# Moving the fifth shifted reading of a bit-trick exp from VectorE to GpSimd, timed beside VectorE's PSUM reads

## The chip, the cores and the metric

The kernel runs on one core of a Trainium2 chip. The metric is the device time of one execution in microseconds (us), lower is better. TensorE is called PE, VectorE DVE, ScalarE ACT and GpSimd POOL in the profile lines.

## The reference

A transformer block with adaptive layer norm: 2048 tokens, width 512, 32 heads of width 16, then a GELU layer of width 1376.

```python
x = A_x                                                  # [1, 2048, 512] bf16
mod = silu(c) @ w_mod                                    # six vectors of 512
h = layernorm(x) * (1 + ca) + sa
q, k, v = split_heads(h @ wqkv, 32)                      # heads of width 16
p = softmax(q @ k.T / 4)                                 # 32 heads, 2048 x 2048 each
x = x + ga * (merge(p @ v) @ wo)
h = layernorm(x) * (1 + cb) + sb
x = x + gb * (gelu(h @ w1 + b1) @ w2 + b2)
```

What matters is the softmax: 32 x 2048 x 2048, or 134 million exponentials, against matmuls of a narrow head width.

## The kernel before

The work is cut into 32 runs. In each, 16 key tiles of 128 keys meet 4 heads x 512 queries. PE computes scores into PSUM in two halves of 128x1024; then each key tile takes one of two ways.

- On ScalarE ("A" tiles): two exps of 128x1024, and then one group of PE products with V.
- On VectorE ("D" tiles): one addition that turns the score into the bits of a bf16 power of two, stored as a 16-bit integer. That is a coarse exp. To smooth it, the integers are also read with four different offsets added ("shifted readings", `sh`, 128x2048), and PE multiplies each of the five readings with its own scaled copy of V. A D tile therefore costs five groups of PE products instead of one.

```python
NPH = 5                                          # readings of a D tile
PH_SH = [round(128 * j / NPH) for j in range(NPH)]       # 0, 26, 51, 77, 102
DKS = (2, 6, 10, 14)                             # key tiles of a run that may go to VectorE
...
def exp_a(qk, r, kt, half):                      # ScalarE
    def go(o):
        n_a[1] += 1
        nc.scalar.activation(out=o.tile, in_=qk.tile, func=ACT.Exp, scale=ESC)
    e = op("ACT", go, 0.92, (qk,), lat=AL, prio=1.0, acq=r_pt, rel=(qk,))
    ...
def exp_d(qk, r, kt, half):                      # VectorE
    first = o_ph[0]
    def go(o):
        n_d[1] += 1
        dst = first.tile[:, half * 2 * QB:(half + 1) * 2 * QB]
        nc.vector.tensor_scalar(out=dst, in0=qk.tile, scalar1=PH_B, scalar2=0.0,
                                op0=ALU.add, op1=ALU.max)         # PSUM -> int16
    e = op("DVE", go, 1.14, (qk, before), lat=DL, prio=0.5, rel=(qk,))
    ...
    pv_op(r, kt, 0, (e,), parts(first), (first,))
    for j in range(1, NPH):
        sh = op("DVE", lambda o, j=j: nc.vector.tensor_scalar(
            out=o.tile, in0=first.tile, scalar1=PH_SH[j], scalar2=None, op0=ALU.add),
            0.6, (e,), lat=DL, prio=2.0, acq=r_sh, rel=(first,))
        pv_op(r, kt, j, (sh,), parts(sh), (sh,))
```

The program contains its own planner. Every operation is given an assumed duration (0.92, 1.14 and 0.6 us above). The planner lists the operations in the order in which they could start by these durations, and emits a fixed instruction order for every engine. Each engine works through its own order and waits at semaphores. So a wrong duration cannot give a wrong result, but it can give an order that does not fit the chip.

Other work sits in the same orders. GpSimd normalises each finished run (`OT`, 128x512), computes the reciprocal standard deviations of the layer norms (`rs`), and scales V for the D tiles (`VX`). VectorE evicts PSUM; PE does the projections and the feed-forward layer. Score buffers `st` are three, exp outputs `pt` nine, D tiles `ph` three, shifted readings `sh` four.

The softmax here doesn't subtract the row's maximum and nothing guards it: scores larger than these inputs give would overflow.

Of the kernel before, what the change touches and what calls it, by code (L numbers as in the profile page):

```python
# [11 lines left out]
ALU = mybir.AluOpType  # L12
ENG = mybir.EngineType
# [58 lines left out]
class Op:  # L72
    count = 0

    def __init__(self, eng, fn, us, deps=(), lat=0.14, prio=5.0, mode=None, kind="", acq=None,
                 rel=(), gate=None):
        self.eng, self.fn, self.us, self.lat, self.prio = eng, fn, us, lat, prio
        self.mode, self.kind, self.acq, self.rel, self.gate = mode, kind, acq, rel, gate
        self.end = None
        self.ready = 0.0  # L80
        self.tile = None
        self.slot = None
        self.kb, self.due, self.extra = 0, 1e9, False
        self.uses = 0
        self.waiters = []
        self.todo = 0
        self.seq = Op.count
        Op.count += 1
        for d in deps:
            if d is None:  # L90
                continue
            if d.end is None:
                d.waiters.append(self)
                self.todo += 1
            else:
                self.ready = max(self.ready, d.end)
        for owner in rel:
            owner.uses += 1


class Plan:
    SLACK = {"PE": 0.10, "DVE": 0.05, "ACT": 0.15, "POOL": 0.05, "SP": 0.05}

    def __init__(self, dyn, later):
        self.later, self.fill_at, self.cool, self.heat, self.until = later, 0.0, 0.0, None, 1e9
        self.free = {e: 0.0 for e in self.SLACK}
        self.lists = {e: [] for e in self.SLACK}
        self.mode, self.tiles, self.now = None, {}, 0.0
        self.bus = 0.0
        self.dyn, self.done, self.fill = dyn, deque(), FILL  # L110

# [13 lines left out]
    def start(self, op):  # L125
        s = max(op.ready, self.pe_start(op) if op.eng == "PE" else self.free[op.eng])
        if op.acq is not None:
            s = max(s, min(op.acq.free))
        if op.eng == "PE" and self.later(op):
            s = max(s, self.fill_at)  # L130
        return s

# [12 lines left out]
    def ahead(self, can):  # L145
# [6 lines left out]
        for s, o in can:  # L152
            end = s + o.us + (0.107 if o.mode[0] != "qk" else 0.0)
            if o.kind == "qkA" or end <= limit:
                keep.append((s, o))
        return keep

    def commit(self, s, o):
# [25 lines left out]
        else:  # L184
            self.free[o.eng] = s + o.us
        o.end = s + o.us + o.lat
        if o.kb:
# [34 lines left out]
def kernel(  # L222
# [29 lines left out]
    ESC = math.log(2.0) / 128.0  # L252
    DKS = (2, 6, 10, 14)
    NPT = 9
    FEW = 2
    MM = 512 / 2400.0
    FIRST_D, D_TIME = 1, 6.0

# [69 lines left out]
    def op(eng, *a, **k):  # L328
        o = Op(eng, *a, **k)
        if eng == "PE":  # L330
            o.due = due_now[0]
            due_now[0] += due_now[1]
        return plan.add(o)
# [179 lines left out]
    def layer_norm(src, deps, mod, mod_dep, hold_z, alloc_h, engines, ps_res, kind, prio,  # L513
# [4 lines left out]
              for t in range(nt)]  # L518
# [3 lines left out]
        za = [op("DVE", lambda o, t=t: apply(ln, z, t, src(t)), 0.33, (z, rs[t // 2]), prio=prio,  # L522
                 rel=(ln,)) for t in range(nt)]
        h = op("POOL", None, 0.0, (rs[0],), lat=0.0, prio=0.0, acq=alloc_h)
# [70 lines left out]
    def make_v(b, cc, kind, acq, eng):  # L595
# [16 lines left out]
        for t in DKS:  # L612
            if t // TPB == b:
# [4 lines left out]
                def scale(o, t=t, vf=vf):  # L618
                    for ph in range(1, NPH):
# [3 lines left out]
                            scalar2=0.0, op0=ALU.mult, op1=ALU.add)  # L623
                got.append(op("POOL", scale, 5 * 0.3, (vf, o_v0[b]), prio=1.0, rel=(vf,)))
        o_v[(cc, b)] = got
# [51 lines left out]
    def qk_op(which):  # L677
# [27 lines left out]
        if which == "D" and half == 0:  # L705
            o_ph[0] = op("POOL", None, 0.0, (), lat=0.0, prio=0.0, acq=r_ph)
        o = op("PE", go, MM, ([o_ph[0]] if which == "D" else []) + [evs[par or 0]] + [o_k[(cc, kb)]], lat=PEL, mode=("qk", half),
               kind="qk" + which, acq=r_st, rel=(qm,),
               gate=(lambda: n_a[0] - n_a[1] < 2) if which == "A" else
               (lambda: n_d[0] - n_d[1] < 2))  # L710
        (exp_a if which == "A" else exp_d)(o, r, kt, half)

    live = {"A": 0, "D": 0}

    def exp_a(qk, r, kt, half):
# [5 lines left out]
        if half == 1:  # L721
            lo = o_e.pop((r, kt, 0))
            o_e.pop((r, kt, 1))
            pv_op(r, kt, 0, (lo, e), lambda: [lo.tile, e.tile], (lo, e))

    def exp_d(qk, r, kt, half):
# [9 lines left out]
        if not half:  # L736
            o_e[(r, kt, 0)] = e
            return

        def parts(o):  # L740
            return lambda: [o.tile[:, h * 2 * QB:(h + 1) * 2 * QB].bitcast(BF16) for h in range(2)]
        pv_op(r, kt, 0, (e,), parts(first), (first,))
        for j in range(1, NPH):
            sh = op("DVE", lambda o, j=j: nc.vector.tensor_scalar(
                out=o.tile, in0=first.tile, scalar1=PH_SH[j], scalar2=None, op0=ALU.add),
                0.6, (e,), lat=DL, prio=2.0, acq=r_sh, rel=(first,))
            pv_op(r, kt, j, (sh,), parts(sh), (sh,))

    def pv_op(r, kt, ph, deps, srcs, owners):
# [43 lines left out]
        o.last_left = lambda: left[r]  # L793
        plan.add(o)

# [5 lines left out]
    def normalise(r):  # L801
# [20 lines left out]
        def d5(o):  # L822
# [5 lines left out]
            out=o.tile, in0=OD.tile, in1=o5.tile, op=ALU.mult), 1.3, (o5,), prio=0.5, acq=r_OT,  # L828
            rel=(OD, o5))

# [83 lines left out]
    def block_tail(b, nt=TPB):  # L914
# [8 lines left out]
        for t in range(nt):  # L923
# [9 lines left out]
                out=x2.tile[:, t, :], in0=y.tile, in1=xr.tile[:, t, :], op=ALU.add), 0.33,  # L933
                (m, xr), prio=1.5, rel=(y,)))
        h, hd, za, trs = layer_norm(lambda t: x2.tile[:, t, :], res_done, modB, o_late["mB"],
# [17 lines left out]
        for t in range(nt):  # L953
            first = None
            for lo, hi in ((0, 4), (4, 8), (8, NF)):
# [11 lines left out]
                out=o.tile, in0=y.tile, in1=x2.tile[:, t, :], op=ALU.add), 0.33,  # L967
                (m, o_late["gb"]), prio=1.5, acq=r_o, rel=(y, x2))
            dma(lambda o, t=t, a=a: nc.sync.dma_start(
# [219 lines left out]
```

## Time and profile before

| | before |
|---|---|
| time, median of 2 runs | 835.43 us (835.25 to 835.62) |
| exps on ScalarE | 778 of 128x1024 |
| PSUM reads for D tiles on VectorE | 246 of 128x1024 (123 tiles) |
| shifted readings on VectorE | 492 of 128x2048 |
| GpSimd busy | 12% |

The page of the profile for the kernel before. Its first part gives busy us, the share of the span and the number of instructions of each engine. The second cuts the span into 40 slices, each digit the busy tenths of one slice; PEclk is the granted PE clock in tenths of full speed. The fourth follows the chain of work that ended last.

```profile
PE 765.7 (91%) x8349; PEld 289.5 (35%) x8430; DVE 770.5 (92%) x1118; ACT 767.8 (92%) x816; POOL 98.4 (12%) x207
...
ACT  3799999898999999999999999999999999998942
POOL 4530221200002100000001100000001000010010
PEclk9999999998999999999999999999999999999999
...
DVE 32%; PE 30%; ACT 29%; issue 7%; DMA 1%; POOL 0%; SPq 0%; POOLq 0%; DVEq 0%; ACTq 0%
```

Busy time by window, kernel before (columns: window, its length, then busy us and number of instructions of PE, PE's weight loads, DVE, ACT and POOL; granted clock, DMA share, GB/s).

```profile
0.00:60.00 60.00, 50.91 (x428) 24.03 (x434) 37.75 (x90) 39.19 (x47) 25.02 (x126) 1.00 0.34 106
60.00:800.00 740.00, 685.67 (x7733) 251.08 (x7810) 714.97 (x995) 715.77 (x753) 71.82 (x78) 0.99 0.09 25
800.00:838.00 38.00, 29.11 (x198) 14.38 (x193) 17.75 (x34) 12.84 (x19) 1.59 (x4) 0.99 0.04 15
```

Three engines are nearly full for 740 us: ACT 96.7%, DVE 96.6%, PE 92.7%. The chain that ended last is split almost evenly among them. GpSimd has hundreds of free microseconds. The change wants these.

Instructions in order of time, kernel before, from 594 us on (columns: start us, duration us, engine, line, operation, output<-inputs, shapes, count, and in brackets the idle time before it and what ended it).

```profile
594.17 0.69 DVE L744 TENSOR_SCALAR sh_9491<-ph_9287 128x2048 int16<-128x2048 int16 x1
...
594.69 1.30 POOL L827 TENSOR_TENSOR OT_9532<-OD_9313,RB_9454 128x512 bf16<-128x512 f32 x1 [21.65 <-DMA RB_9454<-rn]
...
594.77 1.77 DVE L744 TENSOR_SCALAR sh_9502<-ph_9287 128x2048 int16<-128x2048 int16 x1
```

A shift usually takes 0.69 us. The one that begins 0.08 us after a GpSimd normalisation takes 1.77 us: it waits about until GpSimd has ended (594.69 + 1.30 = 595.99) and then needs its own time (it ends at 594.77 + 1.77 = 596.54). All 14 shifts over 0.9 us in this trace overlap or touch such a normalisation. The Trainium skill, "SBUF — State Buffer", section "SBUF: two separate sides", gives the reason: VectorE in a two-port mode and GpSimd share one pair of SBUF ports, and one excludes the other. VectorE's reads of PSUM show no such delay (246 reads, longest 1.23 us).

### The profile page before, as it was taken

How to read it: one execution, taken by the hardware profiler on the slowest of the kernel's cores; microseconds unless marked ns; L12 is line 12 of the kernel's file. 1: busy time of each engine (PE TensorE's matmuls, PEld its weight loads, DVE VectorE, ACT ScalarE, POOL GpSimd, SP SyncE). 2: the span in 40 equal slices, each digit the busy share in tenths (PEclk: the TensorE clock that was granted, in tenths of full speed). 3: DMA queues.
4: the chain of work that ended last, by engine and by line, in shares of the span. 5: the costliest groups of instructions: out<-in, count | busy, mean ns of one | idle time of the engine just before them, and what ended most of it. 6: DMA issues, size and time to landing. Idle time of an engine off the chain costs nothing.

```text
span 837.9 us, 20068 instructions
## 1 busy us (share of the span) xinstructions
PE 765.7 (91%) x8349; PEld 289.5 (35%) x8430; DVE 770.5 (92%) x1118; ACT 767.8 (92%) x816; POOL 98.4 (12%) x207
## 2 busy tenths in 40 slices
PE   8889999999999998998999898999999999999987
PEld 3433333332233332323233332223244444344443
DVE  7849999898999999988999999999999999999982
ACT  3799999898999999999999999999999999998942
POOL 4530221200002100000001100000001000010010
PEclk9999999998999999999999999999999999999999
DMA  6304101001100000000100000000100001000100
GB/s 201 101 1 112 27 16 41 5 23 54 41 15 14 16 15 14 16 20 21 40 16 14 16 14 16 8 28 20 40 15 16 10 12 37 16 28 22 42 7 26
DMA packets 31621, 25.07 MB, mean 30 GB/s; under 512 B 13773, under 2 KB 26926, under 8 KB 31530
## 3 DMA queue, kind: packets, MB, share of 16 engines
q1 hardware_dynamic: 31002, 23.78, 10.2%
q8 instruction: 66, 1.08, 0.5%
q14 instruction: 25, 0.20, 0.1%
q10 hardware_dynamic: 528, 0.00, 0.0%
HBM read 21.16 MB, written 2.61 MB: 28 GB/s over the span
## 4 chain that ended last, share of the span: by engine, by line
DVE 32%; PE 30%; ACT 29%; issue 7%; DMA 1%; POOL 0%; SPq 0%; POOLq 0%; DVEq 0%; ACTq 0%
PE od_13287 L775 1%; DMA blk_178<-in_w_mod_dram 1%; DVE ln_s L485 1%; PE od_11221 L775 1%; PE od_7486 L775 1%; PE od_12207 L775 1%; ACT g_10994 L949 1%; ACT g_7641 L949 1%; ACT g_4693 L949 1%; PE od_5604 L775 1%; PE od_2171 L775 1%; PE od_8961 L775 0%; PE od_10719 L775 0%; PE od_3379 L775 0%; ACT L718 0%
## 5 line engine op out<-in xcount | busy, mean ns | idle before, releaser
L775 PEld LDWEIGHTS <-VEB_92 128*32 128x32 bf16 x640 | 16.5, 96 | 15.8 <-issue 12.7
L775 PEld LDWEIGHTS <-VEB_91 128*32 128x32 bf16 x640 | 16.3, 96 | 16.1 <-issue 12.5
L775 PEld LDWEIGHTS <-VEB_89 128*32 128x32 bf16 x640 | 16.2, 97 | 15.9 <-issue 11.4
L775 PEld LDWEIGHTS <-VEB_90 128*32 128x32 bf16 x640 | 16.4, 96 | 14.4 <-issue 10.5
L942 PEld LDWEIGHTS <-W_83 128*128 128x128 bf16 x176 | 14.1, 97 | 20.3 <-issue 11.5
L700 PEld LDWEIGHTS <-kT_0_121 32*128 32x128 bf16 x128 | 8.0, 91 | 20.6 <-issue 20.1
L700 PEld LDWEIGHTS <-kT_0_109 32*128 32x128 bf16 x128 | 7.0, 91 | 20.0 <-issue 17.8
L700 PEld LDWEIGHTS <-kT_1_122 32*128 32x128 bf16 x128 | 7.0, 91 | 19.2 <-issue 18.7
L700 PEld LDWEIGHTS <-kT_0_113 32*128 32x128 bf16 x128 | 6.6, 91 | 19.1 <-issue 18.7
L700 PEld LDWEIGHTS <-kT_0_117 32*128 32x128 bf16 x128 | 7.0, 91 | 17.8 <-issue 17.2
L700 PEld LDWEIGHTS <-kT_1_114 32*128 32x128 bf16 x128 | 6.3, 91 | 19.7 <-issue 19.1
L700 PEld LDWEIGHTS <-kT_2_111 32*128 32x128 bf16 x128 | 6.8, 91 | 18.3 <-issue 16.5
L700 PEld LDWEIGHTS <-kT_2_123 32*128 32x128 bf16 x128 | 7.1, 91 | 17.2 <-issue 16.8
L700 PEld LDWEIGHTS <-kT_2_119 32*128 32x128 bf16 x128 | 6.9, 91 | 17.6 <-issue 17.3
L700 PEld LDWEIGHTS <-kT_2_115 32*128 32x128 bf16 x128 | 7.0, 91 | 17.2 <-issue 16.3
L700 PEld LDWEIGHTS <-kT_1_110 32*128 32x128 bf16 x128 | 6.8, 91 | 17.8 <-issue 15.4
L700 PEld LDWEIGHTS <-kT_3_120 32*128 32x128 bf16 x128 | 6.6, 91 | 17.7 <-issue 17.1
L700 PEld LDWEIGHTS <-kT_1_118 32*128 32x128 bf16 x128 | 6.3, 91 | 18.6 <-issue 18.2
L700 PEld LDWEIGHTS <-kT_3_124 32*128 32x128 bf16 x128 | 7.3, 91 | 14.8 <-issue 14.3
L700 PEld LDWEIGHTS <-kT_3_112 32*128 32x128 bf16 x128 | 7.0, 91 | 15.7 <-issue 14.3
L700 PEld LDWEIGHTS <-kT_3_116 32*128 32x128 bf16 x128 | 6.4, 91 | 15.1 <-issue 14.3
L501 ACT ACTIVATE blk_292<-st_327,modA 128x512 bf16<-128x512 bf16 x2 | 1.4, 774 | 9.1 <-PE st_327 L533 9.1
(4858 smaller groups left out, 3145.6 us busy)
## 6 DMA issues: line engine op xcount, KB each, us to landing
W_83<-in_B_w_dram SPq DMA_DIRECT2D x1, 1376.0 KB
g_1005<-in_w_mod_dram SPq DMA_DIRECT2D x2, 512.0 KB
xb_127<-in_A_x_dram SPq DMA_DIRECT2D x4, 128.0 KB
blk_174<-in_w_mod_dram SPq DMA_DIRECT2D x1, 512.0 KB
blk_178<-in_w_mod_dram SPq DMA_DIRECT2D x1, 512.0 KB
w_201<-in_A_wqkv_dram SPq DMA_DIRECT2D x1, 512.0 KB
w_205<-in_A_wqkv_dram SPq DMA_DIRECT2D x1, 512.0 KB
xb_210<-in_A_x_dram SPq DMA_DIRECT2D x1, 512.0 KB
```

The lines of the kernel that those rows point to most:

```text
L485: nc.vector.bn_stats(out=st6, in_=src)
L501: nc.scalar.activation(out=dst, in_=src, func=ACT.Identity, bias=mod[:, j:j + 1], scale=mod[:, NC + j:NC + j + 1])
L700: nc.tensor.matmul(out=o.tile[:, g * QB:(g + 1) * QB], lhsT=kT[cc][kb][rows, ko * P:(ko + 1) * P], rhs=qm.tile[rows, par, :] if hb is None ...
L775: nc.tensor.matmul(out=o_od[r].tile[32 * i:32 * i + 32, n * HB:n * HB + w], lhsT=v_tile(kt, ph)[:, c0:c0 + 32], rhs=got[i // 2][:, at:at + ...
L942: nc.tensor.matmul(out=o.tile[:, 0:N], lhsT=W1[:, j, f * P:(f + 1) * P], rhs=h.tile[:, j, 0:N], start=(j == 0), stop=(j == NC - 1))
L949: ge = op("ACT", lambda o: nc.scalar.activation(out=g.tile[:, :, 0:N], in_=g.tile[:, :, 0:N], func=ACT.Gelu_apprx_tanh), 0.1 + 1.2 * nt + ...
```

## The change

The intent: take the fifth reading of each D tile (0.60 us of VectorE) to GpSimd, in two halves of 128x1024. Begin each half only beside a VectorE read of PSUM, which does not need the shared ports and lasts 1.2 us. The plan counts on 1.05 us for a half. With the VectorE time won, up to five instead of four key tiles of a run may go to VectorE, so that ScalarE has fewer exps.

```diff
-    DKS = (2, 6, 10, 14)
+    DKS = (2, 5, 8, 11, 14)
-    FIRST_D, D_TIME = 1, 6.0
+    FIRST_D, D_TIME = 1, 8.0
+    POOL_US, POOL_MIN = 1.05, 0.95
...
+    def piece(first, last, n, e):
+        cols = slice(n * 2 * QB, (n + 1) * 2 * QB)
+        return op("POOL", lambda o: after_dve(nc.gpsimd.tensor_scalar(
+            out=last[0].tile[:, cols], in0=first.tile[:, cols], scalar1=PH_SH[-1], scalar2=None,
+            op0=ALU.add)), POOL_US, (e, last[0]), lat=0.2, prio=1.0, kind="beside", port=True,
+            rel=(first,), gate=lambda: plan.beside(POOL_MIN) or no_more_d())
...
-        for j in range(1, NPH):
+        for j in range(1, NPH - 1):
             sh = op("DVE", ...)
+        two = [piece(first, last, 1, e)]
+        pv_op(r, kt, NPH - 1, [last[1], two[0]], parts(last[0]), (last[0],))
...
+    def after_dve(pool):      # the half waits for the VectorE instruction before the PSUM read
+        own = [i for i in islice(reversed(nc.cur_bb.bb.instructions), 400) if i.engine == ENG.DVE]
+        if len(own) > 1:
+            tc.add_manual_dep(pool.ins, own[1].name, ..., reason="beside")
...
-               gate=(lambda: n_a[0] - n_a[1] < 2) if which == "A" else
+               gate=a_may if which == "A" else
+    def a_may():              # no second score ahead for ScalarE while VectorE waits for one
+        back = n_a[0] - n_a[1]
+        if back >= 1 and live["D"] and n_d[0] == n_d[1]:
+            return sum(f < plan.now for f in r_st.free) > 1
+        return back < 2
```

More of the change, by code (lines that the diff above doesn't have):

```diff
@@ L1 @@
 from collections import deque
+from itertools import islice
 from contextlib import ExitStack
@@ L75, in __init__ @@
     def __init__(self, eng, fn, us, deps=(), lat=0.14, prio=5.0, mode=None, kind="", acq=None,
-                 rel=(), gate=None):
+                 rel=(), gate=None, port=False):
         self.eng, self.fn, self.us, self.lat, self.prio = eng, fn, us, lat, prio
+        self.port = port
         self.mode, self.kind, self.acq, self.rel, self.gate = mode, kind, acq, rel, gate
@@ L109, in __init__ @@
         self.bus = 0.0
+        self.port = {"DVE": 0.0, "POOL": 0.0}
+        self.dve = (0.0, 0.0, True)
         self.dyn, self.done, self.fill = dyn, deque(), FILL
@@ L130, in start @@
             s = max(s, self.fill_at)
+        if op.port and op.us > 0:
+            s = max(s, self.port["POOL" if op.eng == "DVE" else "DVE"])
+        if op.kind == "beside":
+            s = max(s, self.dve[0])
         return s
@@ L156, in ahead, with beside @@
         return keep
+    def beside(self, us):
+        at, end, port = self.dve
+        t = max(at, self.now, self.free["POOL"])
+        if t >= end:
+            nxt = self.pick("DVE")
+            return nxt is None or nxt[0] - t >= us
+        return not port and end - t >= us
     def commit(self, s, o):
@@ L185, in commit @@
             self.free[o.eng] = s + o.us
+            if o.port:
+                self.port[o.eng] = s + o.us
+            if o.eng == "DVE":
+                self.dve = (s, s + o.us, o.port)
         o.end = s + o.us + o.lat
@@ L522, in layer_norm @@
         za = [op("DVE", lambda o, t=t: apply(ln, z, t, src(t)), 0.33, (z, rs[t // 2]), prio=prio,
-                 rel=(ln,)) for t in range(nt)]
+                 rel=(ln,), port=True) for t in range(nt)]
         h = op("POOL", None, 0.0, (rs[0],), lat=0.0, prio=0.0, acq=alloc_h)
@@ L623, in scale @@
                             scalar2=0.0, op0=ALU.mult, op1=ALU.add)
-                got.append(op("POOL", scale, 5 * 0.3, (vf, o_v0[b]), prio=1.0, rel=(vf,)))
+                got.append(op("POOL", scale, 5 * 0.3, (vf, o_v0[b]), prio=1.0, rel=(vf,), port=True))
         o_v[(cc, b)] = got
@@ L724, in exp_a @@
             pv_op(r, kt, 0, (lo, e), lambda: [lo.tile, e.tile], (lo, e))
+    d_last = [None]
+    def piece(first, last, n, e):
[4 more added lines that the diff above has]
+            rel=(first,), gate=lambda: plan.beside(POOL_MIN) or no_more_d())
     def exp_d(qk, r, kt, half):
@@ L737, in exp_d @@
             o_e[(r, kt, 0)] = e
+            to = op("POOL", None, 0.0, (e,), lat=0.0, prio=0.0, acq=r_sh)
+            d_last[:] = [[to, None]]
+            d_last[0][1] = piece(first, d_last[0], 0, e)
             return
@@ L742, in exp_d, with no_more_d @@
         pv_op(r, kt, 0, (e,), parts(first), (first,))
-        for j in range(1, NPH):
+        for j in range(1, NPH - 1):
             sh = op("DVE", lambda o, j=j: nc.vector.tensor_scalar(
                 out=o.tile, in0=first.tile, scalar1=PH_SH[j], scalar2=None, op0=ALU.add),
-                0.6, (e,), lat=DL, prio=2.0, acq=r_sh, rel=(first,))
+                0.6, (e,), lat=DL, prio=2.0, acq=r_sh, rel=(first,), port=True)
             pv_op(r, kt, j, (sh,), parts(sh), (sh,))
+        last = d_last.pop()
+        d_last.append(None)
+        two = [piece(first, last, 1, e)]
+        pv_op(r, kt, NPH - 1, [last[1], two[0]], parts(last[0]), (last[0],))
+    def no_more_d():
+        return not live["D"] and next((0 for r in range(at["D"][0], NR) if shared[r]), None) is None
+    def after_dve(pool):
+        own = [i for i in islice(reversed(nc.cur_bb.bb.instructions), 400) if i.engine == ENG.DVE]
+        if len(own) > 1:
+            tc.add_manual_dep(pool.ins, own[1].name, mybir.DependencyInfo(
+                mybir.DependencyClass.Sync, mybir.DependencyReason.DATA), reason="beside")
     def pv_op(r, kt, ph, deps, srcs, owners):
@@ L793, in pv_op @@
         o.last_left = lambda: left[r]
-        plan.add(o)
+        return plan.add(o)
     for r in range(NR):
@@ L828, in normalise @@
             out=o.tile, in0=OD.tile, in1=o5.tile, op=ALU.mult), 1.3, (o5,), prio=0.5, acq=r_OT,
-            rel=(OD, o5))
+            rel=(OD, o5), port=True)
     o_late = {}
@@ L933, in block_tail @@
                 out=x2.tile[:, t, :], in0=y.tile, in1=xr.tile[:, t, :], op=ALU.add), 0.33,
-                (m, xr), prio=1.5, rel=(y,)))
+                (m, xr), prio=1.5, rel=(y,), port=True))
         h, hd, za, trs = layer_norm(lambda t: x2.tile[:, t, :], res_done, modB, o_late["mB"],
@@ L967, in block_tail @@
                 out=o.tile, in0=y.tile, in1=x2.tile[:, t, :], op=ALU.add), 0.33,
-                (m, o_late["gb"]), prio=1.5, acq=r_o, rel=(y, x2))
+                (m, o_late["gb"]), prio=1.5, acq=r_o, rel=(y, x2), port=True)
             dma(lambda o, t=t, a=a: nc.sync.dma_start(
```

## The prediction

> **What bounds it now.** The busy table: PE 91%, VectorE 92%, ScalarE 92% of 837.9 us; GpSimd 12%. Between 60 and 800 us (the busy times by window) ScalarE is about 97% busy, VectorE 96 to 97%, PE about 93%. The chain of waits is shared almost evenly: VectorE 32%, PE 30%, ScalarE 29%. So three engines are near balance, and the pacer is ScalarE: its 778 exps follow each other every 0.905 us (median start to start; mean 0.926). In that stretch it idles some 24 us before exps, about 14 waiting for PE's scores and 8 for PE's products with V.
>
> **What the change does**, counted from the two instruction orders:
> - Key tiles exponentiated on VectorE go from 123 (of at most 124) to 130 (of at most 155). ScalarE exps: 778 to 764.
> - VectorE: 102 fewer shifted readings of 128x2048 (492 to 390; 0.60 us start to start), 14 more PSUM reads (246 to 260; 1.13 us). Net about -61 + 16 = -45 us.
> - GpSimd: 260 new halves of 128x1024. Estimate from its 128x4096 memset (3.51 us) and 128x128 scalings (0.30 us): about 0.2 us fixed plus 0.85, so 1.05 us each, some 270 us in all. It goes from 12% to about 45% busy.
> - PE: 28 more V products, about +6 us; 14 fewer filler groups, -3 us; changes between kinds of matmul 1242 to 1177. Roughly neutral, in a shorter time.
>
> **What is on the critical path.** VectorE's 45 us are mostly not: it could only turn them into time by taking more key tiles, and takes 7 more. The time should follow ScalarE: 14 exps x 0.905 to 0.926 = 13 us. A VectorE with slack should release score buffers earlier and remove a few us of ScalarE's waits; the fifth reading arriving later, and PE being denser, give some back. Start (about 60 us) and tail (about 35 us) hardly change.
>
> **Contention.** The Trainium skill, "SBUF — State Buffer", section "SBUF: two separate sides", says GpSimd and a two-port VectorE instruction hold the shared port pair exclusively. This trace agrees: every shift over 0.9 us (14 of 492, up to 1.77 instead of 0.68 us) overlaps or touches a GpSimd normalisation, which takes up to 2.39 instead of 1.27 us. The new halves start on the end of the VectorE instruction before a PSUM read (1.22 us long, no shared port), so 1.05 us just fits. I expect an overhang of about 0.1 us on the next shift in many cases, perhaps 10 to 20 us of VectorE time, covered by its 45 us.
>
> **Predicted: 820 us, 811 to 831 (8 in 10).** Chances: faster by over 2% (below about 819) 0.42, within 2% 0.53, slower 0.05.
>
> **What would show it right or wrong in the profile.** ScalarE still 96 to 98% busy from 60 us to the tail, 764 exps at about 0.92 us. VectorE falls to about 88 to 90% of the span. Halves of about 1.05 us, nearly all inside a PSUM read. Median shift still 0.68 us, mean at most 0.8. PE rises to 92 to 94%. ScalarE's waits on PE no longer than before.
>
> **What would make it wrong.** (1) Halves much longer than 1.05 us (16-bit integers on GpSimd), or begun late behind a normalisation that waits for its DMA: shifts then block for 0.5 to 1 us, VectorE is full again, and the time stays near 830 or more. (2) The late fifth reading holds an accumulator or the four shift buffers, so PE's V products and then ScalarE wait: gain below 8 us. (3) PE was the real limit: its work doesn't fall, so the gain is 3 to 5 us. (4) The other way: VectorE's slack also removes most of ScalarE's 24 us of waits and its slower exps, and the time falls to 805 to 812.

## More of the kernel before

The fast runs of the kernel before took 834 to 849 us on different chips. Their time goes with the granted clock, the share of full speed at which the chip let TensorE run (on one chip, 837.1 us at 0.993 and 849.3 us at 0.970). So an experiment is compared only with the runs of the kernel before that were made in turn with it.

## The result, and the profile after

| | before | after |
|---|---|---|
| time, median of 2 runs | 835.43 us | 1073.66 us (1072.69 to 1074.64) |
| exps on ScalarE | 778 | 764 |
| D tiles | 123 | 130 |
| shifts on VectorE | 492 | 390 |
| GpSimd halves | none | 260 |

The ratio is 1.283 (95% interval 1.276 to 1.291). Ratios here are the mean time of one kernel's fast runs over that of the other's of the same rounds, so they are not quite the ratios of the medians.

The page of the profile for the changed kernel: parts one, two, four and five. The groups of part five read: line, engine, operation, output<-inputs, shapes, count | busy us, mean ns of one | idle us of the engine before them, and what ended most of it.

```profile
PE 891.5 (83%) x8514; PEld 297.2 (28%) x8514; DVE 808.6 (76%) x1034; ACT 773.7 (72%) x802; POOL 842.4 (79%) x491
...
ACT  4797686666668797887778786766758787768652
POOL 4567679688788899898897787978988896888760
PEclk9999689785669799998889998888989898989989
...
POOL 40%; PE 29%; DVE 16%; issue 10%; ACT 4%; DMA 1%; SPq 0%; POOLq 0%; DVEq 0%; ACTq 0%
...
L746 ACT ACTIVATE pt<-st 128x1024 bf16<-128x1024 f32 x764 | 732.3, 1029 | 248.1 <-PE st L722 221.8
L758 POOL TENSOR_SCALAR sh<-ph 128x1024 int16<-128x1024 int16 x260 | 744.5, 2882 | 158.2 <-DVE sh L784 103.9
L784 DVE TENSOR_SCALAR sh<-ph 128x2048 int16<-128x2048 int16 x390 | 330.8, 866 | 82.4 <-PE od L829 81.4
L770 DVE TENSOR_SCALAR ph<-st 128x1024 int16<-128x1024 f32 x260 | 316.3, 1217 | 85.2 <-PE st L722 77.1
L829 PE MATMUL od<-sh,VX 128*32 128x512 bf16 (+1 forms) x2624 | 249.5, 377 | 138.2 <-POOL sh L758 125.7
```

The line of L758 is the main reading. A half takes 2.88 us on average, not 1.05. All 260 together take 744.5 us, and GpSimd idles another 158 us before them because each waits for its VectorE instruction. With its other work GpSimd is busy 842 us, and 842 + 158 = 1000 of the 1071 us are accounted for. The kernel before took 835 us in all: GpSimd's work and the waits for its starts no longer fit into that. Correspondingly GpSimd, at 0% of the chain before, now leads it with 40%, and PE waits 125.7 us for its readings (line L829).

Instructions in order of time, changed kernel, VectorE and GpSimd around 405 us.

```profile
404.49 1.15 DVE L784 TENSOR_SCALAR sh<-ph 128x2048 int16<-128x2048 int16 x1
...
405.56 1.21 DVE L770 TENSOR_SCALAR ph<-st 128x1024 int16<-128x1024 f32 x1
...
405.72 2.77 POOL L758 TENSOR_SCALAR sh<-ph 128x1024 int16<-128x1024 int16 x1 [0.63 <-DVE sh L784]
...
406.69 0.68 DVE L784 TENSOR_SCALAR sh<-ph 128x2048 int16<-128x2048 int16 x1
```

The half outlives the PSUM read beside which it was begun (405.56 + 1.21 = 406.77) by 1.7 us, and so meets the shifts after it. The picture of the ports is not simple, though: the shift at 406.69 begins 0.97 us into the half and still takes only 0.68 us. Over the whole trace, among shifts that met a single half, those that began less than 0.7 us into it nearly all ended 1.58 us into it (53 of 60). With 0.68 us of their own, they were thus held until about 0.9 us into it. Those that began 0.8 to 1.6 us into it passed in 0.68 to 0.70 us (means of 0.2 us steps), and 20 of the 24 that began 1.8 to 2.4 us into it took over 0.9 us again. Together the 390 shifts exceed 0.69 us by 71 us (before: 492 shifts, 12 us).

### The profile page after: what moved, and what is told of

The parts are those of the page before. It is cut to its first block, busy times and chain, and to the rows that moved or that the text cites. A ratio compares the mean times of both kernels' runs of the same rounds, so it can differ in the third digit from the quotient of the medians.

```text
span 1070.9 us, 20770 instructions
## 1 busy us (share of the span) xinstructions
PE 891.5 (83%) x8514; PEld 297.2 (28%) x8514; DVE 808.6 (76%) x1034; ACT 773.7 (72%) x802; POOL 842.4 (79%) x491
## 4 chain that ended last, share of the span: by engine, by line
POOL 40%; PE 29%; DVE 16%; issue 10%; ACT 4%; DMA 1%; SPq 0%; POOLq 0%; DVEq 0%; ACTq 0%
POOL sh L758 39%; PE od L829 12%; PE st L722 8%; DVE sh L784 7%; DVE ph L770 4%; ACT pt L746 3%; PE ax L965 2%; PE ax L595 1%; PE ax L996 1%; PE ax L957 1%; PE ax L622 1%; DVE ln_s L507 1%; POOL OT L881 1%; DVE OD L857 1%; DVE g L1000 1%
## 5 line engine op out<-in xcount | busy, mean ns | idle before, releaser
L746 ACT ACTIVATE pt<-st 128x1024 bf16<-128x1024 f32 x764 | 732.3, 1029 | 248.1 <-PE st L722 221.8
L758 POOL TENSOR_SCALAR sh<-ph 128x1024 int16<-128x1024 int16 x260 | 744.5, 2882 | 158.2 <-DVE sh L784 103.9
L784 DVE TENSOR_SCALAR sh<-ph 128x2048 int16<-128x2048 int16 x390 | 330.8, 866 | 82.4 <-PE od L829 81.4
L770 DVE TENSOR_SCALAR ph<-st 128x1024 int16<-128x1024 f32 x260 | 316.3, 1217 | 85.2 <-PE st L722 77.1
L829 PE MATMUL od<-sh,VX 128*32 128x512 bf16 (+1 forms) x2624 | 249.5, 377 | 138.2 <-POOL sh L758 125.7
L722 PE MATMUL st<-qm,kT 32*128 32x512 bf16 x2048 | 332.8, 425 | 26.2 <-ACT pt L746 12.8
L829 PE MATMUL od<-pt,VEB 128*32 128x512 bf16 (+1 forms) x1904 | 166.7, 377 | 0.2 <-DVE OD L857 0.2
L722 PEld LDWEIGHTS <-kT 32*128 32x128 bf16 x2048 | 80.6, 93 | 294.9 <-issue 283.3
L829 PEld LDWEIGHTS <-VX 128*32 128x32 bf16 x2624 | 73.1, 99 | 278.5 <-issue 271.5
L829 PEld LDWEIGHTS <-VEB 128*32 128x32 bf16 x2560 | 71.6, 101 | 70.7 <-issue 56.7
L829 PE MATMUL od<-ph,VEB 128*32 128x512 bf16 (+1 forms) x656 | 63.4, 383 | 2.6 <-DVE OD L857 2.6
```

The costliest lines, as they stand in the source:

```text
L722: nc.tensor.matmul(out=o.tile[:, g * QB:(g + 1) * QB], lhsT=kT[cc][kb][rows, ko * P:(ko + 1) * P], rhs=qm.tile[rows, par, :] if hb is None ...
L758: return op("POOL", lambda o: after_dve(nc.gpsimd.tensor_scalar(out=last[0].tile[:, cols], in0=first.tile[:, cols], scalar1=PH_SH[-1], sca ...
L784: sh = op("DVE", lambda o, j=j: nc.vector.tensor_scalar(out=o.tile, in0=first.tile, scalar1=PH_SH[j], scalar2=None, op0=ALU.add), 0.6, (e, ...
L829: nc.tensor.matmul(out=o_od[r].tile[32 * i:32 * i + 32, n * HB:n * HB + w], lhsT=v_tile(kt, ph)[:, c0:c0 + 32], rhs=got[i // 2][:, at:at + ...
```

## The experiments

Two theories had to be told apart. The first is the **full queue**: the halves are 2.7 times as long as planned, GpSimd has more work than time, and all that it does comes late, the fifth reading as well as normalisations. The second is **blocked shifts**: the halves hold the shared port, and VectorE's own instructions become the slow ones. A third rival was a **bad order**: five tiles a run, the new condition on ScalarE's scores and the longer lead time might be harmful on their own. A further question came up on the way: why halves as short as planned did not give the 15 us that I had predicted.

One caution on correctness. Attention changes the output so little that even versions that fill the fifth reading with a constant passed the comparison with the reference. "Correct" below is therefore weak evidence for the numerics of a reading.

All runs at a glance (medians of all runs; "before" is the kernel before, of the same rounds; the ratio is of fast runs):

| run | this, us | before, us | ratio (95%) |
|---|---|---|---|
| e_dve5: all readings on VectorE | 853.6 | 840.6 | 1.017 (1.011 to 1.023) |
| e_memset: halves are fills | 836.5 | 840.6 | 0.995 (0.989 to 1.001) |
| e_i32: halves are 32-bit additions | 837.9 | 840.6 | 0.999 (0.993 to 1.005) |
| e_port: nobody waits for the halves | 1054.9 | 842.1 | 1.250 (1.243 to 1.258) |
| e_half: half as many halves | 853.4 | 842.3 | 1.012 (1.006 to 1.019) |
| e_tiny: tiny fills, then a fill | 888.7 | 842.3 | 1.056 (1.047 to 1.065) |
| e_queue: a fill, then 42 tiny fills | 1057.6 | 839.5 | 1.264 (1.255 to 1.273) |
| e_pow: 32-bit addition, then two powers | 1018.2 | 841.6 | 1.210 (1.203 to 1.217) |
| b_skip1: before, less PE work | 842.2 | 842.1 | 0.998 (0.992 to 1.004) |
| b_noshift1: before, less VectorE work | 835.2 | 842.1 | 0.989 (0.983 to 0.996) |
| b_noexp: before, 14 exps fewer | 840.4 | 841.6 | 1.000 (0.994 to 1.006) |
| i_skip1: e_i32, less PE work | 834.0 | 842.1 | 0.988 (0.980 to 0.997) |
| i_oldgate: e_i32, old condition | 840.9 | 839.5 | 1.002 (0.998 to 1.007) |
| b_spacing: before, spacing of c_a | 852.8 | 839.5 | 1.017 (1.011 to 1.024) |
| c_a: candidate | 829.0 | 842.3 | 0.983 (0.976 to 0.990) |
| c_b: candidate | 840.7 | 842.3 | 0.996 (0.990 to 1.002) |
| c_c: candidate | 832.1 | 839.5 | 0.992 (0.987 to 0.997) |

### m_forms: what single GpSimd operations take

A separate kernel with nothing but such operations, then VectorE shifts beside some of them.

```python
g.tensor_scalar(out=o16[:, 0:1024], in0=i16[:, 0:1024], scalar1=102, scalar2=None, op0=ALU.add)   # x6, and other sizes and types
g.tensor_tensor(out=o32[:, 0:512], in0=i32[:, 0:512], in1=k32[:, 0:512], op=ALU.add)              # x6
g.tensor_tensor(..., in1=k32[:, 0:1].to_broadcast([P, 512]), op=ALU.add)                           # x6
g.tensor_copy(...); g.memset(...)                                                                  # x6 each
```

> Measures single GpSimd operations by themselves, six of each in a row; the output is zeros (wrong on purpose). Theory of duration: the half of 128x1024 16-bit integers takes about 2.77 us with VectorE idle as well, 512 columns about 1.5 us, 256 columns about 0.85 us (0.2 us fixed and 2.5 ns for each column). Rival, contention: alone it takes about 1.05 us, and the 2.77 us of the changed kernel come from waiting for VectorE. Not known beforehand, and asked here: an exact addition of 512 32-bit integers (two 16-bit ones in each), estimated at 1.3 us from the 1.27 us of the 128x512 float product in the kernel before; a fill of 128x1024, estimated at 1.05 us. The last part runs twenty VectorE shifts of 128x2048 beside six GpSimd operations: if GpSimd holds the shared port for its whole instruction, no shift starts inside one; in the changed kernel shifts begun 0.8 to 1.6 us into a half took 0.68 us, so I expect them to get through in the middle of a half here too.

Groups of GpSimd instructions of m_forms, shapes kept apart (same columns as part five of the page).

```profile
L47 POOL TENSOR_SCALAR o<-i 128x1024 int16<-128x1024 int16 x18 | 54.1, 3004 | 10.0 <-DVE o L38 9.1
...
L47 POOL TENSOR_SCALAR o<-i 128x2048 int16<-128x2048 int16 x6 | 32.2, 5362 | 0.0
...
L47 POOL TENSOR_SCALAR ob<-b 128x1024 bf16<-128x1024 bf16 x6 | 16.6, 2767 | 0.0
L47 POOL TENSOR_SCALAR o<-i 128x512 int16<-128x512 int16 x6 | 8.9, 1487 | 0.0
...
L59 POOL TENSOR_TENSOR o<-i,k 128x512 int32<-128x512 int32 x6 | 7.6, 1260 | 0.0
L79 POOL TENSOR_TENSOR o<-i,k 128x512 int32<-128x512 int32 x6 | 6.2, 1037 | 0.0
L69 POOL COPY o<-i 128x1024 int16<-128x1024 int16 x6 | 6.2, 1036 | 0.0
L73 POOL MEMSET o<- 128x1024 int16 x6 | 5.7, 951 | 0.0
L47 POOL TENSOR_SCALAR o<-i 128x256 int16<-128x256 int16 x6 | 5.1, 847 | 0.0
```

The slow half needs no contention. The 18 additions of the first line are of two kinds: the twelve that met no shift took 2.76 to 2.77 us each, some with VectorE idle throughout, like the bf16 one above; six that ran beside VectorE's shifts took 3.1 to 3.6 us. In five of these six a shift of 0.69 us ran between two of 1.40 us, so it did get through in the middle of a half, as I had expected. From 256 to 512 to 1024 to 2048 columns it takes 0.85, 1.49, 2.77 and 5.36 us, which is 2.5 ns for each column and about 0.2 us fixed. A fill of the same tile takes 0.95 us. I had taken the slope of a fill for that of an addition. L59 and L79 are the same addition of 512 32-bit integers; with the second input a broadcast of one column (L79) it takes 1.04 instead of 1.26 us. Two 16-bit numbers fit in each 32-bit one, so L79 does the work of a half in the 1.05 us of the plan.

### e_dve5, e_memset, e_i32: order or duration?

e_dve5 takes the fifth reading back to VectorE and keeps all other new rules:

```diff
-        for j in range(1, NPH - 1):
+        for j in range(1, NPH):
-        two = [piece(first, last, 1, e)]  ...
```

> Undoes the GpSimd part alone: all five readings on VectorE, the rest of the change kept (five key tiles a run allowed, the new condition on ScalarE's scores, the longer lead time). Theory of duration (GpSimd halves are late): about the time before, 828 to 842 us. Rival, order (the new rules give a bad order by themselves): above 900 us.

Measured: 853.6 us, 1.7% slower than before. That is outside my 828 to 842, but it is 13 us, not 238. The new rules without GpSimd cost a little; they do not explain the loss.

e_memset and e_i32 keep the changed kernel's order on PE, VectorE and ScalarE instruction by instruction and replace only what a half executes:

```diff
-nc.gpsimd.tensor_scalar(out=last[0].tile[:, cols], in0=first.tile[:, cols], scalar1=PH_SH[-1], ...)
+nc.gpsimd.memset(last[0].tile[:, cols], 1)                                          # e_memset
+nc.gpsimd.tensor_tensor(out=last[0].tile[:, cols].bitcast(I32),                     # e_i32
+    in0=first.tile[:, cols].bitcast(I32),
+    in1=shift2[:, 0:1].to_broadcast([P, QB]), op=ALU.add)     # shift2 = 102 * 65537
```

The second rests on the Trainium skill, "GPSIMD Engine Reference", section 4.1 "Engine selection", which states that a GpSimd addition of tensors that are all of one 32-bit integer type is exact, not done in floating point. The output check, by the caution above, does not show exactness.

> Each GpSimd half becomes a fill of the same 128x1024 tile (wrong result on purpose); the order of instructions on PE, VectorE and ScalarE is the same as in the changed kernel. The fill should take about the 1.05 us that the change counts on. Theory of duration: 812 to 832 us, which is what I had predicted for the change. Rival, order: above 900 us all the same. Rival, contention (the shared port, not the length of the halves): 840 to 900 us, as 260 fills still meet VectorE's shifts.

> Each half is computed by GpSimd as an exact addition of 512 32-bit integers to a broadcast constant, two 16-bit numbers at once: a correct result, and the same order on PE, VectorE and ScalarE as in the changed kernel. If it takes about 1.3 us instead of 2.77: theory of duration 825 to 870 us (0.25 us longer than the plan counts on); rival, order: above 900 us; rival, contention: above 900 us, since shifts would be blocked for the whole 1.3 us.

Measured: 836.5 and 837.9 us; e_memset ends just above the 812 to 832 of its theory. The page of e_i32:

```profile
PE 776.7 (93%) x8514; PEld 291.1 (35%) x8514; DVE 729.2 (87%) x1034; ACT 758.4 (91%) x802; POOL 372.5 (45%) x492
...
L748 ACT ACTIVATE pt<-st 128x1024 bf16<-128x1024 f32 x764 | 717.0, 1041 | 35.0 <-PE st L724 21.4
L760 POOL TENSOR_TENSOR sh<-ph,shift 128x512 int32<-128x512 int32 x260 | 274.3, 1057 | 380.9 <-DVE sh L786 220.9
...
L786 DVE TENSOR_SCALAR sh<-ph 128x2048 int16<-128x2048 int16 x390 | 264.4, 703 | 13.6 <-PE od L831 12.7
```

Changing only the instruction behind a half, from 2.88 to 1.06 us, brings 1074 us back to 838. This shows that the slow instruction is the cause, and that the order is not; by which way its length costs the time is the next question. It also shows that the placing works when the length is right: 194 of the 260 halves lie inside a PSUM read (to 0.1 us), and shifts average 0.703 us, as in the kernel before (0.705 us). But neither run is clearly faster than before. The predicted 15 us are missing even with the half as short as assumed. That question is taken up below.

### e_port, e_half, e_tiny, e_queue, e_pow: full queue or blocked shifts?

e_port keeps the slow additions but lets them work on a private tile, and PE takes the unshifted tile for the fifth reading.

```diff
+            out=side, in0=warm[...], scalar1=PH_SH[-1], ...        # private; nobody waits
-        pv_op(r, kt, NPH - 1, [last[1], two[0]], parts(last[0]), (last[0],))
+        pv_op(r, kt, NPH - 1, [e], parts(first), (first,))
-    r_sh = res("sh", 4, ...)
+    r_sh = res("sh", 3, ...)
```

> GpSimd does the same 260 slow additions of 128x1024 16-bit integers, beside VectorE's shifts as before, but on a private tile that nobody waits for; PE reads the unshifted tile in place of the fifth reading (wrong on purpose), and VectorE's shifts keep three buffers. What is left of the slowness is contention for the port and nothing else. Theory of lateness (PE waits for the late fifth reading, and GpSimd as a queue is full): 840 to 900 us, with shifts still at a mean of about 0.85 us. Rival, contention alone: 1000 us or more.

Measured: 1054.9 us, far outside what I had expected of the queue theory and inside the 1000 us or more of the rival. The groups of the page tell why the run cannot decide:

```profile
L758 POOL TENSOR_SCALAR side<-warm 128x1024 int16<-128x1024 int16 x272 | 813.1, 2989 | 70.5 <-DVE sh L783 27.4
L783 DVE TENSOR_SCALAR sh<-ph 128x2048 int16<-128x2048 int16 x408 | 403.9, 1020 | 3.9 <-PE od L828 3.6
...
L956 PE MATMUL ax<-Wo,OT 128*128 128x512 bf16 x112 | 32.2, 408 | 38.9 <-POOL OT L880 38.7
```

The removed wait changed the planner's choice (136 tiles, so 272 halves and 408 shifts). Blocked shifts rose to 137 us of excess over 0.69 us, and GpSimd stayed full, with its normalisations late (PE waits 38.7 us for `OT`). Both theories are alive in it. It refutes only the narrow form of mine, in which nothing but PE's wait for the fifth reading costs time.

e_half and e_tiny went back to the unchanged order. e_half drops every second half. e_tiny makes a half of eighteen tiny fills of 128x1 and a fill of the tile.

```diff
+        return op("POOL", lambda o: None if n else after_dve(nc.gpsimd.tensor_scalar(...      # e_half
+    lambda: [last[0].tile[:, 0:2 * QB].bitcast(BF16)] * 2                                     # PE reads half 0 twice
```
```diff
+            after_dve(nc.gpsimd.memset(tiny[:, 0:1], 0.0))                                    # e_tiny
+            for i in range(17):
+                nc.gpsimd.memset(tiny[:, 1 + i % 15:2 + i % 15], 0.0)
+            nc.gpsimd.memset(last[0].tile[:, cols], 1)
```

> The changed kernel with only the first of the two GpSimd halves of each key tile (130 instead of 260, the same slow 16-bit addition); PE multiplies the first half of the fifth reading twice (wrong on purpose). PE, VectorE and ScalarE keep their order. GpSimd's work falls from about 850 us to about 470. Theory of the full queue (what costs is that GpSimd's own work, some 850 us and the waits for its start, no longer fits the 835 us, and everything GpSimd does comes late): the loss nearly vanishes, 835 to 870 us. Rival, contention: shifts are still blocked by each remaining half as often, so about half the loss stays, 930 to 970 us.

> The changed kernel with each half made of eighteen tiny fills of 128x1 and one fill of the tile (wrong on purpose): GpSimd is as busy as with the slow half, an estimated 18 x 0.1 + 0.95 = 2.75 us each, but holds the port for long only in the one fill. The order on PE, VectorE and ScalarE is kept. Theory of the full queue: 1000 to 1090 us, with shifts at a mean below 0.80 us. Rival, contention: below 900 us.

e_half measured 853.4 us, as the full queue expects: GpSimd's busy time falls to 477 us (56%), and of the loss of 238 us only 11 are left although each remaining half is still 2.90 us long. e_tiny's 888.7 us lies in the rival's range (below 900), but it did not test what it was made for. The tiny fills took less than estimated, so that its GpSimd is not full. From the page of e_tiny:

```profile
PE 791.0 (90%) x8435; PEld 296.6 (34%) x8514; DVE 788.0 (89%) x1034; ACT 767.5 (87%) x802; POOL 505.2 (57%) x5171
...
L789 DVE TENSOR_SCALAR sh<-ph 128x2048 int16<-128x2048 int16 x390 | 324.7, 856 | 10.6 <-PE od L834 9.9
```

By accident this is the best measure of the blocked shifts. The fill now begins some 0.6 us later and meets the next shift. Shifts average 856 ns, nearly the 866 ns of the changed kernel, with an excess of 67 against 71 us, at the same order. With GpSimd at 57% that costs 46 us (888.7 against 842.3). In the changed kernel nearly the same excess comes with a loss of 238 us. So, if the same excess costs the same there, blocked shifts are worth about 50 us, and the rest needs another cause.

e_queue was to fill GpSimd without holding the port, by 42 tiny fills after the fill:

```diff
+            after_dve(nc.gpsimd.memset(last[0].tile[:, cols], 1))
+            for i in range(42):
+                nc.gpsimd.memset(tiny[:, i % 16:1 + i % 16], 0.0)
```

> The changed kernel with each half made of one fill of the tile, begun where the change wants it, and then 42 tiny fills of 128x1 (wrong on purpose): at the 0.043 us each that they took net in the run with eighteen, some 0.95 + 1.8 = 2.75 us of GpSimd for each half, as with the slow addition, but the port is held for long only in the first 0.95 us. PE waits for the fill alone; PE, VectorE and ScalarE keep their order. Theory of the full queue: 980 us or more, with shifts at a mean of 0.80 us or less. Rival, blocked shifts: 835 to 870 us.

The time came out as the queue theory said, 1057.6 us, but for the wrong reason, so it counts for nothing:

```profile
L788 DVE TENSOR_SCALAR sh<-ph 128x2048 int16<-128x2048 int16 x390 | 481.0, 1259 | 13.1 <-PE od L833 12.5
```

A row of tiny fills does keep VectorE from the port. Shifts average 1.26 us, the longest 4.17 us, and the excess of 224 us by itself matches the loss.

e_pow replaces the filler by powers. In the 17 earlier traces of whole programs all 26 shifts that began inside a GpSimd power (of the layer norms' `rs`) ran in 0.67 to 0.69 us, so these powers did not hold the port for long.

```diff
+            after_dve(nc.gpsimd.tensor_tensor(... int32 addition of e_i32 ...))
+            for k in (4, 2):
+                nc.gpsimd.tensor_tensor(out=spin[:, 4:4 + k], in0=spin[:, 0:k], in1=mhalf[:, 0:k], op=ALU.pow)
```

> The changed kernel with the short 32-bit addition for each half (1.04 us, correct result), followed on GpSimd by two powers of 128x4 and 128x2 on constants, about 1.7 us in which the port is not held: about 2.75 us of GpSimd for each half, as with the slow addition. PE, VectorE and ScalarE keep their order. Theory of the full queue: 980 to 1070 us. Rival, blocked shifts: about 840 us and at most the sum by which shifts exceed 0.69 us (in e_tiny 67 us of such excess made 52 us), so 840 to 890 us.

Measured: 1018.2 us. From the page of e_pow:

```profile
POOL 62%; PE 18%; DVE 11%; issue 6%; ACT 3%; DMA 0%; POOLq 0%; DVEq 0%; ACTq 0%
...
L766 POOL TENSOR_TENSOR spin<-spin,mhalf 128x4 f32<-128x4 f32 (+1 forms) x520 | 540.4, 1039 | 20.4
...
L792 DVE TENSOR_SCALAR sh<-ph 128x2048 int16<-128x2048 int16 x390 | 309.8, 813 | 64.5 <-PE od L837 63.6
...
L762 POOL TENSOR_TENSOR sh<-ph,shift 128x512 int32<-128x512 int32 x260 | 283.1, 1089 | 45.1 <-DVE sh L792 20.3
```

Here the addition is the short one, and the order is the changed kernel's. GpSimd is merely kept busy for another 2.1 us a half ((283.1 + 540.4) / 260 = 3.17 us together, somewhat more than the 2.88 us of the slow half). The time rises from about 838 to 1018 us. The premise held: of 260 shifts that began inside a power only 9 took over 0.9 us. The excess over all shifts is 51 us, less than in e_tiny with its 46 us of loss, while the loss here is 177 us. The full queue is thus shown as the larger part, and blocked shifts as a smaller one that a late GpSimd brings with it.

### b_skip1, b_noshift1, b_noexp, i_skip1, i_oldgate: where did the expected 15 us go?

The first three take work from one engine of the kernel before and leave all orders as they are. Their outputs are wrong, which doesn't matter for the times.

```diff
+            if ph == 1 and not first and left[r] > 0:
+                parts = ()                                 # b_skip1, i_skip1: no products of the second reading
```
```diff
-            sh = op("DVE", lambda o, j=j: nc.vector.tensor_scalar(
+            sh = op("DVE", lambda o, j=j: None if j == 1 else nc.vector.tensor_scalar(   # b_noshift1
```
```diff
+        gone = half == 1 and kt == 7 and r in range(2, 30, 2)                             # b_noexp: 14 exps
+            if not gone:
                 nc.scalar.activation(out=o.tile, in_=qk.tile, func=ACT.Exp, scale=ESC)
```

> The kernel before, without PE's products of the second reading with V (some 123 groups of four matmuls at about 0.21 us, 26 us of PE; wrong on purpose); VectorE and ScalarE do what they did, in the same order. Theory, PE is the pacer: 15 to 25 us less. Rival, ScalarE is the pacer (my prediction's step): less than 6 us less. Rival, VectorE: less than 6 us less.

> The kernel before, without VectorE's second reading (123 shifts of 0.60 us, 74 us of VectorE; PE multiplies the first reading in its place, wrong on purpose); PE and ScalarE do what they did, in the same order. Theory, PE is the pacer: 0 to 8 us less. Rival, VectorE is the pacer: 30 us less or more.

> The kernel with the fast GpSimd halves (32-bit additions), without PE's products of the second reading (130 groups, about 28 us of PE; wrong on purpose). If PE is what ate the expected 15 us: 810 to 822 us, that is 15 to 27 us less than with them (838). If ScalarE or VectorE paces: 832 us or more.

> The kernel before without 14 of ScalarE's 778 exps, spread over 14 runs (PE multiplies the first half of those tiles twice, wrong on purpose); nothing else changes, in order or work. If ScalarE paces, as my prediction had it: 13 us less (1.5%). If the saving is given back as waits of ScalarE for scores, as with the short GpSimd halves: 0 to 5 us less.

Measured against the kernel before: some 27 us less of PE (its products with V are busy 295.3 us instead of 322.8) gave nothing clear (0.998), 64 us less of VectorE (busy 706.9 us instead of 770.5) gave 1.1%, and 14 exps less of ScalarE gave nothing (1.000, interval 0.994 to 1.006, five rounds). So my theory for b_skip1, that PE paces, fell as well. The third is the exact step of my prediction, done alone. The page of b_noexp:

```profile
L721 ACT ACTIVATE pt<-st 128x1024 bf16<-128x1024 f32 x764 | 716.5, 1045 | 41.7 <-PE st L700 27.9
```

ScalarE idles 41.7 us before its exps. In the kernel before the same idle time, summed over its 778 exps, is 26.3 us. The exps themselves are busy 716.5 us instead of 726.3: 9.8 us saved came back as 15.4 us of waiting, mostly for scores of PE. The difference, 5.6 us, is that by which this profiled run happens to be longer than that of the kernel before (spans of 843.5 us at a granted clock of 0.978 and 837.9 us at 0.989); over all runs the two times are equal. The kernel before has no single pacer: its chain passes through VectorE, PE and ScalarE in nearly equal parts, and each engine's order is fixed. In e_i32 the same happened: ScalarE's idle time before exps is 35.0 us. PE's additional products may have some part in it: i_skip1, without some 27 us of PE's products, reaches 0.988 where e_i32 reached 0.999. But the intervals overlap, the comparison crosses two sets of rounds, and the 810 to 822 us expected if PE were the cause were not reached (834.0 us).

i_oldgate tests whether the new condition on ScalarE's scores gave the saving back:

```diff
-               gate=a_may if which == "A" else
+               gate=(lambda: n_a[0] - n_a[1] < 2) if which == "A" else
```

> Short 32-bit halves, and only the new condition on ScalarE's scores undone (774 exps on ScalarE, 250 reads on VectorE). If that condition gave back the expected gain by interrupting ScalarE: 824 to 832 us, and fewer than 65 exps that begin after a wait (87 with the condition, 54 in the kernel before). If not: 835 us or more.

Half of the expectation came true: with the old condition only 45 exps begin after a wait, against 84 by the same count in e_i32. But the waits are longer (34.8 us in sum), and the time is 840.9 us, no better. The condition is not what ate the gain.

### Candidates: c_a, c_b, c_c, and b_spacing

With the short half, several constants of the planner (lead time, spacing of projections and feed-forward work between the exps) can be chosen anew. I took three settings with short schedules by the program's own planner out of some 280. c_a has the old condition, `TAIL` 200 for 185 and `HEAT` 1.2 for 1.3; c_b keeps the new condition with `D_TIME` 11, `FEW` 1, `TAIL` 170, `CB` 44 and `HEAT` 1.2; c_c has the old condition and wider changes. b_spacing gives the kernel before c_a's two constants and nothing on GpSimd.

```diff
-    TAIL, CB = 185, 49                       # c_a, b_spacing
+    TAIL, CB = 200, 49
-HEAT = 1.3
+HEAT = 1.2
```

> Candidate with a correct result: the 32-bit halves, the old condition on ScalarE's scores, and other spacing of the side work; 776 exps on ScalarE, 248 reads on VectorE. If the new condition on ScalarE's scores is what gave back the expected gain, about 825 us (1.5% below before). If not, within 1% of before.

> Candidate with a correct result: the 32-bit halves and the new condition kept, a longer lead time for VectorE's tiles and other spacing of the side work; 770 exps on ScalarE, 254 reads on VectorE. Expected 828 to 838 us, within 1% of before; clearly faster only if lead time is what cost the gain.

> Candidate with a correct result: short 32-bit halves, the old condition on ScalarE's scores, wider spacing of the side work; 776 exps on ScalarE, 248 reads on VectorE. Expected 820 to 830 us, 1.5 to 2.5% below before.

> The kernel before with the two spacing constants of candidate c_a, nothing on GpSimd. If c_a's 1.7% comes from the spacing alone: about 828 us. If it needs the short GpSimd halves: 836 us or more.

c_a took 829.0 us against 842.3 (0.983, interval 0.976 to 0.990), and c_c 832.1 against 839.5 (0.992). Both beat both kernels, by less than 2%; c_b did not. c_c and c_b ended just above the ranges expected of them. The page of c_a:

```profile
L748 ACT ACTIVATE pt<-st 128x1024 bf16<-128x1024 f32 x776 | 724.3, 1048 | 21.5 <-PE st L724 12.2
L760 POOL TENSOR_TENSOR sh<-ph,shift 128x512 int32<-128x512 int32 x248 | 260.3, 1052 | 371.2 <-DVE sh L786 221.1
```

c_a has only two exps fewer than the kernel before but 5 us less idle time before them (21.5 against 26.3). Its gain is thus not the one I had predicted; it goes with an order that has fewer waits. Part of it also goes with the clock: c_a's runs were granted 0.983 to 1.0, the fast runs of the kernel before 0.970 to 0.993, and at 0.983 each the two took 833.1 and 842.3 us (1.1%). b_spacing shows that the constants by themselves make the kernel before 1.7% slower, and i_oldgate shows that the halves and the old condition by themselves give nothing. Which waits the combination removes was not pursued. Since settings were picked for their outcome, a small part of the 1.7% may be selection.

## Why the prediction was wrong, point by point

- **"So 1.05 us each, some 270 us in all."** This is the step that failed. A half takes 2.77 us alone and 2.88 us in the kernel; 260 take 744.5 us. The estimate took its slope from a fill (3.51 us for 4096 columns), and its check, a 128x128 scaling of 0.30 us, is too short to show a slope. The mis-sized term makes GpSimd's sum 842 us busy plus 158 us of waits for its starts, more than the whole time before. Shown by e_i32 and e_memset, which change only this instruction and are back at 838 and 837 us.
- **GpSimd "from 12% to about 45% busy".** Measured 79%. With the short halves it is 45%.
- **"What would make it wrong", case (1), "Halves much longer than 1.05 us (16-bit integers on GpSimd)".** The case was named and its consequence undersized: I wrote that VectorE would be full again and the time near 830 us or more. VectorE fell to 76% busy instead. The larger loss came from GpSimd's queue (e_pow: 1018 us with short additions and a busy GpSimd; e_half: 853 us with half of the slow additions), and some 50 us from blocked shifts (e_tiny).
- **"The time should follow ScalarE: 14 exps x 0.905 to 0.926 = 13 us."** Also wrong, and independent of the first error. b_noexp takes these 14 exps away and changes nothing; ScalarE waits 15 us more. With the half as short as assumed the change is at 0.999. Even with the duration right, 820 us would have been missed by some 15 us.
- **"VectorE's 45 us are mostly not on the path."** Supported: 64 us less of VectorE gave 1.1% in b_noshift1.
- **Contention.** The exclusion between normalisations and shifts was read correctly, and beside a PSUM read a half of 1.05 us does fit: in e_i32 shifts average 0.703 us.
- **Clock.** I expected nothing of it. The mean granted PE clock of the profiled run is 0.88 in the changed kernel and 0.87 to 0.90 in the runs of e_port, e_queue and e_pow, with PE busy 82 to 84% of the span, against 0.98 to 0.99 in the runs near 840 us, with 91 to 93%. The same 8514 matmuls are busy 891.5 us in the changed kernel and 776.7 us in e_i32. Whether the lower clock only follows from PE's waiting, and how much of the loss is owed to it, was not measured by itself.

What stays open: the exact division of the 238 us between full queue, blocked shifts and PE clock, and which waits cancel a saving on one engine of the balanced kernel. A plan made with the slow half's true 2.77 us was not run either.

## What to carry to other kernels

Before handing work to an idle engine, measure that very instruction, in its type and size, on that engine, and sum the engine's whole load with it: an engine at 12% has room for 260 operations of 1 us but not of 2.8 us. When a profile shows several engines above 90% and a chain split evenly among them, do not count the time saved on one of them as time saved; remove exactly that work in a run and look where the wait goes. An experiment meant to hold one thing still must be checked for it in its own profile, as e_queue's shifts show.

## What the Trainium skill lacked or had wrong

- "GPSIMD Engine Reference", section 4.1 "Engine selection", calls one-input elementwise operations on GpSimd roughly line-rate. The one-input addition measured here takes 2.5 ns a column, which is 3.0 cycles at the 1.2 GHz of that page's specifications, for 16-bit integers and bf16 alike (2.77 us for 128x1024). A copy of the same tile takes 1.04 us and a fill 0.95 us. The page's 2.6 cycles per element, section 3.1, are for the two-input addition; taken for this one they give an estimate of 2.2 us, and would have warned me.
- "SBUF — State Buffer", section "SBUF: two separate sides", says that the shared port pair is held for the whole instruction. For the 16-bit addition this is not what the trace shows: shifts that began 0.8 to 1.6 us into a half of 2.77 us ran in 0.68 to 0.70 us, and those before were held only until about 0.9 us. For the 128x512 product it holds (1.77 instead of 0.69 us).
- The same page does not say that GpSimd powers leave the port free (251 of 260 shifts begun inside a 128x4 or 128x2 power stayed under 0.9 us), nor that a row of 128x1 fills keeps VectorE off it (shifts at a mean of 1.26 us, up to 4.17 us).
- No page has it that a 32-bit addition on GpSimd is faster with a broadcast column as second input: 1.04 instead of 1.26 us for 128x512.
